# A three-stage kernel on one core: the low half of M taken by VectorE in block 0, and the conversion of the weights re-ordered

## The chip, the cores and the metric

One core of one Trainium2 chip runs the whole program. The time is in device microseconds of one execution, and lower is better. TensorE (PE) multiplies; ScalarE (ACT) and VectorE (DVE) work element by element; SyncE (SP) issues every transfer of this kernel. TensorE's clock is granted at one of two levels, 1.2 or 2.4 GHz; the profile gives it as 0.50 or 1.00.

## The reference

```python
scores  = scale * x @ state^T                 # B=8, H=8, S=512, Ns=32, D=64
xread   = softmax(scores) @ state             # tokens read the state
sread   = softmax(scores^T) @ x               # the state reads the tokens
x = concat([xread, sread]) as 4608 rows of 512
x = relu(x @ w_in)**2 @ w_out                 # first layer pair, 512 -> 2048 -> 512
y = elu(x @ w2_in) @ w2_out                   # second layer pair, 512 -> 2048 -> 512
```

The activations are 32-bit floats. The four weight matrices come as 64-bit floats, and the kernel makes 32-bit ones of them on the chip.

## The kernel before

**Precision.** TensorE multiplies numbers that are cut to fewer bits (fp32r). Each operand is therefore held as two such parts, a high one (`HI`) and a low one (`LO`, what the high one leaves over), and each product is made of three matmuls of 128x512: HI·LO, HI·HI, LO·HI (`mm3`, lines 168 to 172). `split` (line 174) makes the two parts: ScalarE copies the high part, VectorE subtracts it from the source.

**Blocks and steps.** The tokens are worked on in eight blocks of 512, one for each entry of the batch. Blocks 0 to 3 are the single stage. A block has 16 steps f, and each step (`s1_step`) makes a tile h of 128 hidden units by 512 tokens with six matmuls (`h<-at,m`), then relu and square on ScalarE (`relu2`: r, g and the high part of gs) and the low part of gs on VectorE. Two steps later (`LAG` is 2) `out_step` multiplies that gs with the output weights by twelve matmuls (`acc<-gs,v`). Blocks 4 to 7 are the pair stage: it begins with steps that make h for block 4 (`h_step`, line 737) and works in fewer products over pairs of blocks. The second layer pair comes last.

**M.** Instead of making x for a block and multiplying it with w1, the kernel multiplies state with w1 (M, in four groups g of four steps; `emit_m`, `m_heads`: 8 short matmuls `mp<-w,st`) and the attention weights with M. A group of M needs two units of w1, and steps 4g to 4g+3 need the group. In blocks 1 to 7 `split` makes M's two parts. In block 0 TensorE makes the low one: the high part is multiplied by minus one (tile `minus`) and added to the bank in which M stands, and ScalarE copies what is left (lines 374 to 376).

**Conversion of the weights.** Beside the blocks, `next_conv` advances a list of units (`converting`): w1 and v1 (8 units each, in block 0), then combinations of v1 (`sums_v1`), then w2 and v2 (`conv_pair`). A unit of `convert` (line 222) has two ScalarE instructions of 128x1024 (lines 232 and 234), three VectorE ones (236, 237, 240), and for v1 a high copy on ScalarE (256) and a subtraction on VectorE (258). Its transfers go through SyncE's queue. `wf` is the split result of a later unit (281, 282), written back to memory. What has not been converted when block 3 ends is done at once (`while busy or converting`, line 706).

**Order.** Each engine runs its instructions in a fixed order, which a scheduler writes down from the order of the code and from `issue_after` hints: inside such a context the instructions that go to the engine of the named instruction come behind it on that engine. `gate` and `pace` hold such instructions: `pace` is the last step's relu.

**The beginning.** `begin_block` does block 0's attention while the first weights arrive; `busy_pe(n)` puts n matmuls that compute nothing (`idle`) into TensorE's order. Two matmul records stand for one such matmul.

Of the kernel before, what the change touches and what calls it, by code (L numbers as in the profile page):

```python
# [8 lines left out]
F32 = mybir.dt.float32  # L9
F32R = mybir.dt.float32r  # L10
I32 = mybir.dt.int32
U32 = mybir.dt.uint32
AF = mybir.ActivationFunctionType
# [96 lines left out]
def attn_mlp_kernel(ctx: ExitStack, tc: tile.TileContext, xt, xn, st, w1, v1, w2, v2, outx, outs):  # L110
# [57 lines left out]
    def mm3(ps, w, x, first, last):  # L168
# [2 lines left out]
        mm(ps, w[HI], x[HI], start=False, stop=False)  # L171
        mm(ps, w[LO], x[HI], start=False, stop=last)  # L172

    def split(hi, lo, src):
        copy = nc.scalar.activation(out=hi, in_=src, func=AF.Copy)  # L175
        nc.vector.tensor_tensor(out=lo, in0=src, in1=hi.bitcast(F32), op=ALU.subtract)  # L176
        return copy

    x2d = [dram.tile([P, KC, S if b < B else NST], F32, name=f"x2d{b}", tag=f"x2d{b}") for b in range(B + 1)]
# [1 line left out]
    if True:  # L181
        ident = const.tile([P, P], F32, name="ident")
        make_identity(nc, ident)
        minus = const.tile([P, P], F32R, name="minus")
        nc.scalar.activation(out=minus, in_=ident, func=AF.Copy, scale=-1.0)
        stf = sf_p.tile([P, KC, NST], F32, name="stf", tag="stf")


# [33 lines left out]
        def convert(name, i, out):  # L222

            t = raw.pop((name, i))
            low, high = t[..., 0], t[..., 1]
            bits = out.bitcast(I32)
            after = pace if name in ("w2", "v2") else gate  # L230
            with tc.issue_after(after[0].ins) if after else nullcontext():
                nc.scalar.activation(out=out, in_=high.bitcast(F32), func=AF.Prelu, scale=2.0 ** -112, alpha=NEGATIVE)
            with tc.issue_after(gate[-1].ins) if gate else nullcontext():
                taken[:] = [nc.scalar.activation(out=low, in_=low.bitcast(U32), func=AF.Copy, scale=2.0 ** -29)]
            yield
            nc.vector.tensor_scalar(out=out, in0=out, scalar1=CLAMP, scalar2=-NEGATIVE * CLAMP, op0=ALU.min, op1=ALU.max)
            nc.vector.tensor_single_scalar(out=bits, in_=bits, scalar=3, op=ALU.logical_shift_left)
            yield
            for r in range(2) if (name, i) == ("w1", 1) else [slice(0, 2)]:
                added[name, i] = nc.vector.tensor_tensor(out=bits[:, r], in0=bits[:, r], in1=low[:, r], op=ALU.add)  # L240
# [8 lines left out]
        def conv_v1(i):  # L249
            v = conv_p["cv"].tile([P, 2, 512], F32, name="cv", tag="cv")  # L250
            yield from convert("v1", i, v)
            next_pair(reading)
            d = dram.tile([P, 2, 512], F32, name=f"d_v1{i}", tag=f"d_v1{i}")
            nc.sync.dma_start(out=d, in_=v)
            t = wo_p.tile([P, 2, 2, DM], F32R, name=f"v1_{i}", tag="wo")
            nc.scalar.activation(out=t[:, :, HI], in_=v, func=AF.Copy)
            yield
            nc.vector.tensor_tensor(out=t[:, :, LO], in0=v, in1=t[:, :, HI].bitcast(F32), op=ALU.subtract)
            for r in range(2):
                wd["v1", 2 * i + r], wo_t["v1", 2 * i + r] = d[:, r], t[:, r]  # L260
# [54 lines left out]

        v1d = {}
        wo_t = {}
        pieces = [("w1", 0), ("w1", 1), ("v1", 0), ("v1", 1)]
        for i in range(2, 8):
            pieces += [("w1", i), ("v1", i)]  # L320
        pairs2 = [(name, j) for name in ("w2", "v2") for j in range(HF)]
        converting = pieces + [("f1", j) for j in range(HF)] + pairs2[:IN_SINGLE]
        of_units = lambda units: [(name, i, r) for name, i in units for r in range(2)]
# [23 lines left out]
        def next_piece():  # L347
            next_conv(converting[0][0] in ("w1", "v1"))

        m_t, minus_copy = {}, []  # L350

        def heads(ps, b, x, ks=range(KC)):

# [5 lines left out]
        def m_heads(ps, b, g, ks):  # L359
            heads(ps, b, lambda k, r: half[g, k // 2][r, k % 2, :], ks)  # L360

        def emit_m(b, g):

            ps = [ps_aux.tile([P, 512], F32, name=f"mp{b}_{g}_{e}", tag="aux") for e in range(2)]
            m_heads(ps, b, g, range(KC))
            split_m(b, g, ps)

        def split_m(b, g, ps):
            for e in range(2):
                t = m_p.tile([P, 2, 512], F32R, name=f"m{b}_{g}{e}", tag="m")  # L370
                if b:
                    split(t[:, HI], t[:, LO], ps[e])
                else:
                    nc.scalar.activation(out=t[:, HI], in_=ps[e], func=AF.Copy)
                    mm(ps[e], minus, t[:, HI], start=False, stop=True, skip_group_check=True)
                    minus_copy[:] = [nc.scalar.activation(out=t[:, LO], in_=ps[e], func=AF.Copy)]
                m_t[b, g, e] = t

        A = {}
# [19 lines left out]
        def begin_block():  # L399

            act, tt, after = nc.scalar.activation, nc.vector.tensor_tensor, lambda i: tc.issue_after(i.ins)
            pss = [ps_aux.tile([P, 512], F32, name=f"sc0_{e}", tag="aux") for e in range(2)]
            with busy_pe(14):
                heads(pss, 0, lambda k, r: xt_t[0][r, k, :])
            load_xn(0)
            for queue in (reading, loading, reading):
# [15 lines left out]
            neg = nc.vector.tensor_scalar_mul(mx, mx, -SCALE)  # L422
            busy_pe(4)
            units = [conv_w1(i) for i in range(2)]
            del converting[:2]
            gate[:] = [last]
            next(units[0])
            gate.clear()
# [9 lines left out]
            next(units[1])  # L438
            gate[:] = taken
            unit = conv_v1(0)  # L440
            del converting[0]
            next(unit)
            gate.clear()
            A[0] = dict(t=t, e2=e2, z2=z2)
# [4 lines left out]
            next(units[0], None)  # L449
            last = added["w1", 0]  # L450
            m_heads(mps, 0, 0, (0, 1))
            busy_pe(6)
            a2t = A[0]["a2t"] = at_p.tile([P, ST, 2, P], F32, name="a2t0", tag="a2t")
            tp = ps_t.tile([P, ST, 2, P], F32, name="tp0", tag="pt")
            for s in range(ST):
# [11 lines left out]
            for c in range(2):  # L467
                for s in range(ST):
                    nc.tensor.transpose(atf[:, c, s * P:(s + 1) * P], back[:, c, s], ident)
            with after(last):  # L470
                next(units[1])
            next(units[1], None)
            m_heads(mps, 0, 0, (2, 3))
            operand(0)
            with after(copies[0]):
                split_m(0, 0, mps)
            next(unit)
            gate[:] = [copies[0], minus_copy[-1]]
            second = conv_v1(1)
            del converting[0]  # L480
            next(second)
            busy.append((second, "v1"))
            gate[:] = gate[1:]
            next(unit)
            next(unit, None)

        def at_soft1(b):

# [141 lines left out]
        def busy_pe(n):  # L630

            t = ps_s1.tile([P, 512], F32, name="idle", tag="s1")
            for i in range(n):
                last = mm(t[:, i % 4 * P:(i % 4 + 1) * P], ident, ident, start=True, stop=True, skip_group_check=True)
            return tc.issue_after(last.ins)
# [10 lines left out]
        for b in range(SINGLE):  # L646
            bg = {i: later.pop(i, []) for i in range(FC + LAG)}

            def at(i, fn, *a):
                bg[i].append(lambda: fn(*a))  # L650

            nb = b + 1
            if b == 0:
                for i in range(FC - 1):
                    at(i, next_piece)
                    at(i, next_conv, False)
                at(0, gate.clear)
                at(3, emit_m, 0, 1)
                at(7, emit_m, 0, 2)
                at(11, emit_m, 0, 3)  # L660
                at(1, at_sread, 0)
                at(2, at_srt, 0)
                at(2, load_x, 1)
            else:
                at(1, emit_m, b, 1)
                at(5, emit_m, b, 2)
                at(9, emit_m, b, 3)
                for i in range(18):
                    for _ in range(int(('111111211211111100', '111111212211211100')[b == 1][i])):
                        at(i, next_conv)  # L670
            at(13, emit_m, nb, 0)
            if nb < SINGLE:
# [501 lines left out]
```

## Time and profile before

| | |
|---|---|
| median of three runs | 1321.7 us (1320.56 to 1325.08) |
| the profiled execution, its time | 1325.68 us |
| its span, from the first to the last instruction | 1323.9 us |
| mean granted clock | 0.996 |
| PE, DVE, ACT busy in the span | 98%, 71%, 63% |

A row of a timeline gives the start in us from the span's start, the duration, the engine, the line, the operation, the tiles (out<-in), the shape and the count. In brackets stands how long the engine had been idle before, and what ended the wait. Successive starts are closer together than durations, since the next instruction begins before the last one has drained.

### The profile page before, as it was taken

The numbers are of one execution on the slowest core, as the hardware profiler recorded it, in microseconds if no ns is written. First come the engines' busy times: TensorE is split into PE (matmuls) and PEld (weight loads), VectorE is DVE, ScalarE is ACT, GpSimd is POOL, SyncE is SP. The second block draws the span as 40 slices with busy tenths as digits, with TensorE's granted clock in tenths as the row PEclk, the third lists the DMA queues.
The fourth block names the chain that finished last, engine by engine and source line by source line (L and its number), as shares of the span: only waits on it lengthen the run. The fifth ranks groups of instructions, "written<-read, shape, count | busy, mean of one in ns | idle before, by whom it ended". The sixth has DMA issues, their size and how long they took to land.

```text
span 1323.9 us, 19412 instructions
## 1 busy us (share of the span) xinstructions
PE 1302.3 (98%) x6972; PEld 1039.9 (79%) x6972; DVE 942.0 (71%) x1324; ACT 840.3 (63%) x1358; POOL 0.7 (0%) x6
## 2 busy tenths in 40 slices
PE   7999999999899999999999999999999999999999
PEld 5677777777577777778988888788888888888888
DVE  5984768787968965895856963689546984568645
ACT  6995677777776566654657743675446843666444
POOL 0000000000000000000000000000000000000000
PEclk8999999999999999999999999999999999999999
DMA  9788767778843663589676677777786677778733
GB/s 376 276 309 308 265 238 253 293 269 304 317 139 106 226 196 120 151 273 334 260 248 196 191 209 240 247 190 213 207 288 195 207 209 222 211 201 283 229 118 112
DMA packets 135408, 305.39 MB, mean 231 GB/s; under 512 B 14352, under 2 KB 28688, under 8 KB 132240
## 3 DMA queue, kind: packets, MB, share of 16 engines
q1 hardware_dynamic: 135312, 304.14, 70.6%
q8 instruction: 56, 0.92, 0.3%
q14 instruction: 40, 0.33, 0.1%
HBM read 227.54 MB, written 76.55 MB: 230 GB/s over the span
## 4 chain that ended last, share of the span: by engine, by line
PE 78%; DVE 9%; DMA 6%; ACT 2%; issue 2%; SPq 0%; ACTq 0%; DVEq 0%
PE x L43 19%; PE X L43 13%; PE z L43 9%; PE Z L43 6%; PE y L43 3%; PE acc L170 3%; PE h L170 3%; PE Y L43 3%; PE h L172 3%; PE h L171 3%; PE acc L172 3%; PE acc L171 3%; PE mp L357 2%; PE as L43 2%; PE hs L43 1%
## 5 line engine op out<-in xcount | busy, mean ns | idle before, releaser
L176 DVE TENSOR_TENSOR gp<-g,gp 128x512 fp32r<-128x512 f32 (+1 forms) x224 | 212.0, 955 | 106.4 <-ACT gp L175 105.4
L175 ACT ACTIVATE gp<-g 128x512 fp32r<-128x512 f32 (+1 forms) x224 | 187.2, 843 | 154.8 <-PE x L43 74.9
L43 PE MATMUL x<-gp,wr 128*128 128x512 f32 x1152 | 273.5, 391 | 1.4 <-DVE gp L176 1.4
L43 PEld LDWEIGHTS x<-gp,wr 128*128 128x128 f32 x1152 | 214.8, 188 | 53.0 <-DVE gp L176 4.1
L43 PE MATMUL X<-xf,wr 128*128 128x512 f32 x768 | 186.9, 390 | 1.0 <-ACT u L960 1.0
L43 PEld LDWEIGHTS X<-xf,wr 128*128 128x128 f32 x768 | 143.4, 188 | 32.9 <-ACT u L960 2.5
L43 PE MATMUL z<-gp,wr 128*128 128x512 f32 x576 | 133.5, 390 | 0.0
L43 PEld LDWEIGHTS z<-gp,wr 128*128 128x128 f32 x576 | 107.9, 188 | 23.5 <-issue 0.8
L956 DVE SCALAR_TENSOR_TENSOR g<-r,g 128x512 f32<-128x512 f32 x96 | 64.0, 689 | 62.8 <-ACT r L955 62.8
L170 PE MATMUL acc<-gs,v 128*128 128x512 f32 x256 | 103.7, 405 | 2.3 <-DVE gs L592 1.6
L170 PE MATMUL h<-at,m 128*128 128x512 f32 x256 | 102.5, 400 | 0.5 <-ACT g L746 0.5
L172 PE MATMUL h<-at,m 128*128 128x512 f32 x256 | 100.5, 394 | 0.0
L171 PE MATMUL h<-at,m 128*128 128x512 f32 x256 | 100.4, 393 | 0.0
L172 PE MATMUL acc<-gs,v 128*128 128x512 f32 x256 | 100.1, 391 | 0.0
L171 PE MATMUL acc<-gs,v 128*128 128x512 f32 x256 | 99.7, 389 | 0.0
L43 PE MATMUL Z<-xf,wr 128*128 128x512 f32 x384 | 97.6, 389 | 0.0
L954 ACT ACTIVATE r<-g 128x512 f32<-128x512 f32 x96 | 57.6, 625 | 60.3 <-DVE g L1004 43.6
L81 DVE TENSOR_TENSOR g<-g,g 128x1024 f32<-128x1024 f32 x72 | 87.5, 1220 | 0.8
L43 PEld LDWEIGHTS Z<-xf,wr 128*128 128x128 f32 x384 | 72.0, 188 | 15.2 <-DVE g L1010 0.3
L955 ACT ACTIVATE r<-r 128x512 f32<-128x512 f32 x136 | 81.5, 621 | 0.7
L170 PEld LDWEIGHTS acc<-gs,v 128*128 128x128 f32 x256 | 48.0, 188 | 29.8 <-issue 11.7
L43 PE MATMUL y<-gp,wr 128*128 128x512 f32 x288 | 68.6, 389 | 0.0
(169 smaller groups left out, 2002.1 us busy)
## 6 DMA issues: line engine op xcount, KB each, us to landing
wr<-f_v SPq DMA_DIRECT2D x288, 256.0 KB, 3.1
wr<-f_w SPq DMA_DIRECT2D x224, 256.0 KB, 3.0
f_v<-wf SPq DMA_DIRECT2D x40, 512.0 KB, 3.4
raw_w<-in_w_dram SPq DMA_DIRECT2D x32, 512.0 KB, 5.7
raw_v<-in_v_dram SPq DMA_DIRECT2D x32, 512.0 KB, 6.6
f_w<-wf SPq DMA_DIRECT2D x24, 512.0 KB, 3.3
wr<-p_v SPq DMA_DIRECT2D x48, 256.0 KB, 3.5
xt<-in_xt_dram SPq DMA_DIRECT2D x8, 1024.0 KB, 6.8
```

Source lines behind the costliest of these rows:

```text
L43: nc.tensor.matmul(ps, wk[a], xk[b], start=start and k == 0 and i == 0, stop=last and k == len(w) - 1 and i == 2, skip_group_check=True)
L81: return lambda jj: tt(out=out[jj], in0=a[jj], in1=b[jj], op=ALU.subtract)
L170: mm(ps, w[HI], x[LO], start=first, stop=False)
L171: mm(ps, w[HI], x[HI], start=False, stop=False)
L172: mm(ps, w[LO], x[HI], start=False, stop=last)
L175: copy = nc.scalar.activation(out=hi, in_=src, func=AF.Copy)
L176: nc.vector.tensor_tensor(out=lo, in0=src, in1=hi.bitcast(F32), op=ALU.subtract)
L357: mm(ps[e][32 * k:32 * k + 32, :], st_t[b][r, k, :], x(k, r), start=True, stop=True)
L954: act(out=r, in_=h, func=AF.Relu, scale=-1.0)
L955: act(out=r, in_=r, func=AF.Exp, scale=-1.0)
L956: nc.vector.scalar_tensor_tensor(out=out, in0=r, scalar=-1.0, in1=h, op0=ALU.add, op1=ALU.max)
```

## The change

Five things change. In block 0, as in the others, `split` makes both parts of M: the eight matmuls with `minus`, the tile itself and ScalarE's eight copies of a low part are gone, and VectorE gets eight subtractions. The unit that was converted ahead of step 0 as a second one of v1 now comes in its turn. All conversion copies of ScalarE, not those of w2 and v2 alone, stand behind the last step's relu. The high copies of v1's units 3 and 7 go to VectorE. The idle matmuls are dealt out otherwise (12, 4, 4, 4 for 14, 4, 6), M's heads take k in the order 2, 3, 0, 1, and block 1 advances the conversion 24 times instead of 20.

```diff
     def split(hi, lo, src):
         copy = nc.scalar.activation(out=hi, in_=src, func=AF.Copy)
-        nc.vector.tensor_tensor(out=lo, in0=src, in1=hi.bitcast(F32), op=ALU.subtract)
+        lows[:] = [nc.vector.tensor_tensor(out=lo, in0=src, in1=hi.bitcast(F32), op=ALU.subtract)]
...
-        minus = const.tile([P, P], F32R, name="minus")
-        nc.scalar.activation(out=minus, in_=ident, func=AF.Copy, scale=-1.0)
...
-            after = pace if name in ("w2", "v2") else gate
+            after = gate or pace
...
-            with tc.issue_after(gate[-1].ins) if gate else nullcontext():
+            with tc.issue_after(after[-1].ins) if after else nullcontext():
...
-            nc.scalar.activation(out=t[:, :, HI], in_=v, func=AF.Copy)
+            if i % 4 == 3:
+                nc.vector.tensor_copy(out=t[:, :, HI], in_=v)
+            else:
+                nc.scalar.activation(out=t[:, :, HI], in_=v, func=AF.Copy)
...
-        pieces = [("w1", 0), ("w1", 1), ("v1", 0), ("v1", 1)]
+        pieces = [("w1", 0), ("w1", 1), ("v1", 0)]
         for i in range(2, 8):
-            pieces += [("w1", i), ("v1", i)]
+            pieces += [("w1", i), ("v1", i - 1)]
+        pieces += [("v1", 7)]
...
-            m_heads(ps, b, g, range(KC))
+            m_heads(ps, b, g, (2, 3, 0, 1))
...
-                if b:
-                    split(t[:, HI], t[:, LO], ps[e])
-                else:
-                    nc.scalar.activation(out=t[:, HI], in_=ps[e], func=AF.Copy)
-                    mm(ps[e], minus, t[:, HI], start=False, stop=True, skip_group_check=True)
-                    minus_copy[:] = [nc.scalar.activation(out=t[:, LO], in_=ps[e], func=AF.Copy)]
+                split(t[:, HI], t[:, LO], ps[e])
...
-            with busy_pe(14):
+            with busy_pe(12):
...
-            busy_pe(6)
+            with after(last):
+                busy_pe(4)
...
             with after(last):
+                busy_pe(4)
                 next(units[1])
...
-            next(unit)
-            gate[:] = [copies[0], minus_copy[-1]]
-            second = conv_v1(1)
-            del converting[0]
-            next(second)
-            busy.append((second, "v1"))
-            gate[:] = gate[1:]
+            with after(lows[0]):
+                next(unit)
+            gate[:] = lows
             next(unit)
             next(unit, None)
+            gate.clear()
...
-                    for _ in range(int(('111111211211111100', '111111212211211100')[b == 1][i])):
+                    for _ in range(int(('111111211211111100', '222222111211211100')[b == 1][i])):
```

The scheduler moves more than the diff shows. Line numbers of the changed kernel are a few lower or higher for the same statement. Here is TensorE's order in the beginning, before the change, from the last matmul of block 0's scores (`sc`) to the first of its M (`mp`):

```order
L357 MATMUL sc_1_176<-xt_165,st_163 32x512
L634 MATMUL idle<-ident 128x128 x3
L420 MATMUL pt<-ident,sc_210 128x128 x8
L634 MATMUL idle<-ident 128x128 x7
L457 MATMUL tp_271<-ident,e_212 128x128 x3
L357 MATMUL mp_0_0_251<-w_0_235,st_163 32x512
```

And with the change:

```order
L361 MATMUL sc_1_174<-xt_163,st_161 32x512
L631 MATMUL idle<-ident 128x128 x10
L419 MATMUL pt<-ident,sc_206 128x128 x8
L631 MATMUL idle<-ident 128x128 x2
L456 MATMUL tp_265<-ident,e_208 128x128 x2
L361 MATMUL mp_0_0_247<-w_0_231,st_161 32x512
```

Seven of the idle matmuls (the new calls hint at a VectorE instruction, which orders nothing on TensorE) have moved ahead of the transposes `pt`, on which the softmax of block 0 waits.

VectorE's order in the changed kernel shortly before M's third group (`m_20`, `m_21`), where `cv` and `v_3` belong to units of v1, `w_5` to one of w1, `t` and `z` to the softmax of block 1:

```order
L257 CAST v_3_626<-cv 128x2x512
L237 TENSOR_SCALAR w_5_628<-w_5_628 128x1024
L261 TENSOR_TENSOR v_3_626<-cv,v_3_626 128x2x512
L489 TENSOR_REDUCE m_634<-t_573 128x32
L589 TENSOR_TENSOR gs<-g,gs 128x512
L490 TENSOR_TENSOR t_573<-t_573,m_634 128x1024
L240 ISA w_5_628<-raw_w_363,w_5_628 128x2048
L236 TENSOR_SCALAR cv<-cv 128x1024
L497 TENSOR_REDUCE z_691<-t_573 128x32
L237 TENSOR_SCALAR cv<-cv 128x1024
L240 ISA cv<-raw_v_157,cv 128x2048
L178 TENSOR_TENSOR m_20_685<-mp_2_0_675,m_20_685 128x512
```

Before, VectorE had no part in M in block 0; its order from the same unit of w1 on was:

```order
L237 TENSOR_SCALAR w_5_646<-w_5_646 128x1024
L396 STREAM_TRANSPOSE t_591<-sc_0_595 128x512
L396 STREAM_TRANSPOSE t_591<-sc_1_596 128x512
L240 ISA w_5_646<-raw_w_379,w_5_646 128x2048
L592 TENSOR_TENSOR gs<-g,gs 128x512
L258 TENSOR_TENSOR v_4_644<-cv,v_4_644 128x2x512
```

The low part of M now stands behind the whole of a v1 unit's three instructions, and the unit of w1 that M needs behind more of the softmax.

ScalarE's order where block 3 ends, before the change (`oo`, `o`: the block's result; `wf`: units of the conversion that are left; L746: the first relu of the pair stage, tile h_3575):

```order
L622 ACTIVATE oo<-acc 128x512
L622 ACTIVATE o<-acc 128x512
L281 ACTIVATE wf<-tf 128x2x256
L175 ACTIVATE m_10_3608<-mp_1_0_3598 128x512
L175 ACTIVATE m_11_3611<-mp_1_1_3599 128x512
...
L175 ACTIVATE m_20_3680<-mp_2_0_3670 128x512
L175 ACTIVATE m_21_3683<-mp_2_1_3671 128x512
L281 ACTIVATE wf<-cv 128x2x256
L281 ACTIVATE wf<-tf 128x2x256
L746 ACTIVATE g_3582<-h_3575 128x512
```

And with the change, where that relu is line 742:

```order
L619 ACTIVATE oo<-acc 128x512
L619 ACTIVATE o<-acc 128x512
L742 ACTIVATE g_3573<-h_3566 128x512
L746 ACTIVATE g_3573<-g_3573 128x512
L177 ACTIVATE gp<-g_3573 128x512
L742 ACTIVATE g_3573<-h_3580 128x512
L491 ACTIVATE t_3418<-t_3418 128x1024
L177 ACTIVATE m_10_3599<-mp_1_0_3589 128x512
```

The first relu of the pair stage has moved from behind thirteen other instructions to right behind the block's result.

## Rows read from the trace of the kernel before

**Rows 1.** The page: busy us (share of the span) xinstructions.
```profile
PE 1302.3 (98%) x6972; PEld 1039.9 (79%) x6972; DVE 942.0 (71%) x1324; ACT 840.3 (63%) x1358; POOL 0.7 (0%) x6
```

**Rows 2.** Windows: us, busy PE, PEld, DVE, ACT, POOL (xcount), clock, DMA share, GB/s.
```profile
20.00:30.00 10.00, 7.38 (x20) 4.17 (x21) 6.89 (x10) 7.65 (x11) 0.00 (x0) 0.53 1.02 409
...
70.00:80.00 10.00, 10.00 (x50) 8.38 (x49) 9.92 (x14) 10.00 (x16) 0.00 (x0) 1.00 0.85 302
```

**Rows 3.** TensorE's timeline, the beginning up to the first output product.
```profile
1.35 6.02 PE L634 MATMUL idle<-ident 128*128 128x128 f32 x28 [1.35 <-POOL ident masks.py:199]
...
10.12 1.73 PE L634 MATMUL idle<-ident 128*128 128x128 f32 x14
...
21.73 2.52 PE L357 MATMUL mp<-w,st 64*32 64x512 f32 x8 [1.92 <-DVE w L240]
25.14 0.79 PE L375 MATMUL mp<-m,minus 128*128 128x512 f32 x1 [0.89 <-ACT m L374]
25.73 0.63 PE L170 MATMUL h<-at,m 128*128 128x512 f32 x1
...
35.63 0.50 PE L170 MATMUL acc<-gs,v 128*128 128x512 f32 x1 [1.58 <-DVE gs L592]
```

**Rows 4.** TensorE's timeline: first products with M's groups 1, 2 and 3.
```profile
48.67 0.39 PE L170 MATMUL h<-at,m 128*128 128x512 f32 x1
...
68.10 0.39 PE L375 MATMUL mp<-m,minus 128*128 128x512 f32 x1
68.33 0.39 PE L170 MATMUL h<-at,m 128*128 128x512 f32 x1
68.55 0.39 PE L375 MATMUL mp<-m,minus 128*128 128x512 f32 x1
...
88.59 0.39 PE L170 MATMUL h<-at,m 128*128 128x512 f32 x1
```

**Rows 5.** ScalarE's timeline, one step with a unit of w1.
```profile
30.66 0.60 ACT L587 ACTIVATE r<-h 128x512 f32<-128x512 f32 x1 [0.56 <-PE h L172]
31.16 1.20 ACT L232 ACTIVATE w<-raw_w 128x1024 f32<-128x1024 f32 x1
32.23 0.64 ACT L589 ACTIVATE g<-r 128x512 f32<-128x512 f32 x1
...
33.27 1.13 ACT L234 ACTIVATE raw_w<-raw_w 128x1024 int32<-128x1024 uint32 x1
34.29 1.05 ACT L256 ACTIVATE v<-cv 128x1024 fp32r<-128x1024 f32 x1
```

**Rows 6.** VectorE's timeline, a unit of v1 and the low part of a gs.
```profile
27.64 0.69 DVE L236 TENSOR_SCALAR cv<-cv 128x1024 f32<-128x1024 f32 x1 [2.32 <-ACT cv L232]
28.37 0.69 DVE L237 TENSOR_SCALAR cv<-cv 128x1024 int32<-128x1024 int32 x1
29.20 1.23 DVE L240 CUSTOM_DVE_ANT_0 cv<-raw_v,cv 128x2048 uint16<-128x2048 uint16 x1
30.34 1.22 DVE L258 TENSOR_TENSOR v<-cv,v 128x1024 fp32r<-128x1024 f32 x1
...
34.90 0.68 DVE L592 TENSOR_TENSOR gs<-g,gs 128x512 fp32r<-128x512 f32 x1
```

**Rows 7.** TensorE's timeline from block 3's end to the fifth step of block 4.
```profile
346.14 1.25 PE L519 MATMUL tp<-ident,e 128*128 128x128 f32 x8 [0.46 <-DVE m L176]
348.30 2.05 PE L357 MATMUL mp<-w,st 64*32 64x512 f32 x16 [0.91 <-ACT a2t L520]
351.81 1.06 PE L357 MATMUL mp<-w,st 64*32 64x512 f32 x8 [1.45 <-DVE m L176]
353.38 0.50 PE L170 MATMUL h<-at,m 128*128 128x512 f32 x1 [0.51 <-ACT g L746]
...
354.97 1.04 PE L357 MATMUL mp<-w,st 64*32 64x512 f32 x2
```

**Rows 8.** ScalarE's timeline, the first relu of the pair stage.
```profile
352.75 0.58 ACT L746 ACTIVATE g<-h 128x512 f32<-128x512 f32 x1
```

More of the change, by code (lines that the diff above doesn't have):

```diff
@@ L172, in mm3 @@
         mm(ps, w[LO], x[HI], start=False, stop=last)
+    lows = []
     def split(hi, lo, src):
         copy = nc.scalar.activation(out=hi, in_=src, func=AF.Copy)
-        nc.vector.tensor_tensor(out=lo, in0=src, in1=hi.bitcast(F32), op=ALU.subtract)
+        lows[:] = [nc.vector.tensor_tensor(out=lo, in0=src, in1=hi.bitcast(F32), op=ALU.subtract)]
         return copy
@@ L348, in next_piece @@
             next_conv(converting[0][0] in ("w1", "v1"))
-        m_t, minus_copy = {}, []
+        m_t = {}
         def heads(ps, b, x, ks=range(KC)):
@@ L424, in begin_block @@
             units = [conv_w1(i) for i in range(2)]
-            del converting[:2]
+            del converting[:3]
             gate[:] = [last]
@@ L476, in begin_block @@
                 split_m(0, 0, mps)
-            next(unit)
-            gate[:] = [copies[0], minus_copy[-1]]
-            second = conv_v1(1)
-            del converting[0]
-            next(second)
-            busy.append((second, "v1"))
-            gate[:] = gate[1:]
+            with after(lows[0]):
+                next(unit)
+            gate[:] = lows
             next(unit)
             next(unit, None)
+            gate.clear()
         def at_soft1(b):
@@ L656, in attn_mlp_kernel @@
                     at(i, next_conv, False)
-                at(0, gate.clear)
                 at(3, emit_m, 0, 1)
```

## The prediction

> **What bounds the kernel now.** The page comes first: TensorE (PE) is busy for 98% of the span [rows 1], so a change can gain only where TensorE waits, where its clock is low, or where it is spared work. The windows by stage and TensorE's timeline show three such places. The first is the beginning: between 20 and 30 us the granted clock is 0.53, that is mostly the 1.2 GHz level [rows 2], after a time in which TensorE had little to do; it waits 1.92 us for a unit of w1, 0.89 for M's high copy, and 1.58 before the first output product at 35.63 [rows 3]. The second is the rest of block 0, where from 70 to 80 us VectorE is busy for 9.92 and ScalarE for 10.0 of 10 us while TensorE has no gap [rows 2]: there neither of the two can take on work without TensorE soon waiting for it. The third is the end of block 3. From 345.7 to 353.4 TensorE waits four times, 3.33 us in all, and the two short groups of M between take longer than their work [rows 7].
>
> **The change, the beginning.** A step's ScalarE work comes from its successive starts: relu 0.50, first conversion copy 1.07, g and gs 1.04 together, second copy 1.02, and for v1 a high copy of 0.95 to 1.05 [rows 5]. On VectorE a unit takes 0.73, 0.83 and 1.14, v1's subtraction 1.13 to 1.22, a low part of 512 columns 0.68 or a little less [rows 6]. A TensorE product starts every 0.225 us at full clock [rows 4]; at the lower level I take 0.45.
>
> The idle matmuls ahead of the scores are four records fewer, at 0.215 each [rows 3]: 0.85 us earlier at the most. I take 0.4, since the transfer of x then decides. Against that, fourteen more records stand before the transposes `pt`, 0.124 each at the later rate [rows 3], 1.7 us, part of it a wait for the copy anyway: `pt` and the softmax come some 0.9 later than now. VectorE's two steps of the first v1 unit, about 1.2 us, which stood between the softmax and the second unit of w1, now stand behind M. These three cancel to within 0.3 us, so M's heads start near 21.7 as now, and the first product h stands where the matmul with `minus` stood, at 25.0 instead of 25.73 [rows 3].
>
> From there: twelve products of steps 0 and 1 at 0.45 end at 30.2, the read of the state takes 1.1, and the six of step 2, mostly at full clock, end at 32.8. The first output product needs gs of step 0: relu at 28.65 (eight products after 25.0), 2.6 of ScalarE, 0.6 of VectorE, 31.9; and v1's high copy, 32.2. So it starts at 32.8 instead of 35.63. ScalarE is now the slow one. From 28.65 it has four steps without a gap, 4 x 3.63 + 2 x 0.95 = 16.4, then M's copy, and the first product with M's group 1 comes at 45.6. Before, it is at 48.67 [rows 4]. By the orders of the two programs 37 output products stand ahead of it before and 39 with the change; at equal work that is 48.67 + 2 x 0.225 - 45.6 = **3.5 us gained**.
>
> **The rest of block 0.** ScalarE is spared six more low copies (0.5 each) and two high copies of v1; VectorE gets six low parts (0.6 to 0.68) and the two high copies. No row shows such a copy on VectorE: its nearest are L236, one source and the same 1024 columns in 0.69, and L258, two sources in 1.22 [rows 6]. I take 0.69, since the copy has one source. The Trainium skill (VectorE: DVE Perf Modes, the perf-mode tier table) says that in 32 bits one-source operations between SBUF tiles run at twice the rate of two-source ones; with 1.22 the third group of M would come 0.55 later.
>
> By its order VectorE has in steps 4 to 7 four gs (2.6), two units of w1 (5.4), two of v1 (7.7), a high copy (0.7), two low parts of M (1.3) and about 6.5 of block 1's softmax: some 24 us against 18.6 of TensorE (72 products and the short groups). TensorE has output products in reserve, but it works them off. Going down the orders row by row with the durations above: the high copy of v1's unit 3 is ready at 60.4, wanted at 60.0; gs of step 7 0.6 late; M's group 2 at 67.95, where 96 output products have been done, against 78 at 68.33 before [rows 4]: 68.33 + 18 x 0.225 - 67.95 = 4.4 gained. Then `m_20`'s low part, queued behind a v1 unit's addition, holds TensorE for 1.6 (70.45 instead of 68.85), and behind it stand all further products. ScalarE's next four steps, from 71.55, have no gap: 4 x 3.63, two copies of 0.5 for the transposed weights, one of 0.5 of the operand, v1's 0.95 and M's 0.5 make 17.5, and group 3 comes at 89.0, with 136 output products done instead of 125 at 88.59 [rows 4]: 88.59 + 11 x 0.225 - 89.0 = 2.1. Conversion ends around 95 in both, from where TensorE alone decides; one more low part behind the last v1 unit leaves **1.8 us gained** at the end of block 0. Bounds: -2, if the hand-overs add a few tenths at each of a dozen waits, and 4.4, if the lag at group 3 is made up.
>
> **The end of block 3.** Before, the first relu of the pair stage runs at 352.75 [rows 8], though its product was ready when block 3 ended; it stands behind thirteen instructions, the leftover conversion among them. All banks for h are then full, so TensorE stands from 345.7 to 353.4, with 7.7 us for eight transposes (about 0.8), one full group of M (1.1) and half of another (1.06 by its row): 4.75 lost. Two groups are also cut in two, as the row at 354.97 shows (1.04 for two records, where the whole group needs 1.1) [rows 7]; in the new order they stand whole, 2.0 more. With the change the relu runs right behind the block's result. What is late next is M's group 1, behind an exponential on ScalarE, and its low parts behind two sums and a leftover piece on VectorE: I find waits of 0.4 to 1.9, and take 1.9. **4.85 us gained**; bounds 2 (the leftover still delays the softmax of block 5) and 6.4.
>
> **At nothing.** The 24 idle matmuls in all are as many as before. Block 1's four further advances lie in a stretch where ScalarE and VectorE are idle for a third and a fifth of the time. The raw words of v1's first four units are loaded before step 0 in both, and each later one is requested at least one step, 4 us, ahead of its copy; if that cover were gone, a transfer costs ScalarE what it waits.
>
> **The sum.** 1.8 + 4.85 = 6.7 us from the profiled execution's 1325.7 (its span 1323.9 and 1.8 around it): 1319.0. That execution is 0.3% above the median of the three runs shown, so the same share of the median gives 1321.7 x 1319.0 / 1325.7 = **1315 us**. About 0.3%, 4 us, is what a measurement of this kernel can tell from no change.
>
> **The rivals.**
> - VectorE and ScalarE eat up the whole gain of block 0. For it speak the full windows [rows 2]; against it the six low copies less on ScalarE. At the bound of -2 the sum is 2.85 and the time 1319. 0.17.
> - The clock rises later. In the beginning TensorE now has a gap between the idle matmuls and the scores, and only four idle records between the transposes and M instead of fourteen. If the scores, the twenty records and `pt` run at 1.2 GHz, they take some 3.5 longer, and the softmax of block 0 comes that much later: 6.7 - 3.5 leaves 3.2, 1318.5. Rows 3 speak against it, as 24 records still run without a gap before the scores. The Trainium skill (TensorE: Matmul & The Clock Gate, Part 4: PE-mode transpose) says that transposes do not count as activity for the clock; by that rule it would fall earlier here. No row tells transposes from the rest, though the clock did fall after a stretch that had mostly those. 0.10.
> - The end of block 3 does not get shorter: the wait moves from the relu to a transfer of the last converted pieces, whose tiles the pair stage's tiles replace. Before, such a transfer was one of the things waited for. Then 1.8 are left, 1320. 0.13.
> - Slower: VectorE decides all of block 0. Its work from gs of step 0 to group 3 is about 59 us; from 31.9 without idling it ends at 91. To lose 0.3% it must eat 4.85 + 4 on top of the 2.1 counted there, which is when it idles for 16% of that time, waiting for ScalarE in turn: then about 1326. Before, in 70 to 80 us, it idled for under 1% [rows 2]. 0.08.
>
> **How the numbers follow.** The forecast has 0.52, with 1311 to 1318 as its own range, nearly all of it faster by over 0.3%. The first two rivals reach below 1317.7 in about a third of their cases, which adds 0.08. So faster 0.58, within 0.3% 0.33, slower 0.09. The range goes from 1310.5, where block 0 gains 4.4 and the end of block 3 6.4, to 1321.5, where block 0 loses 2 and the end of block 3 gives 2; that leaves about 0.2 out.
>
> **What would show it.** In the profile of the changed kernel: the first output product near 32.8 and the first with M's group 1 near 45.6; a wait of TensorE for VectorE's low part of M in block 0 of one to two us; VectorE over 95% busy from 45 to 88; no gap of several us at the start of the pair stage, and its first relu within 2 us of block 3's result. The prediction is wrong if the first output product comes after 35, if block 0's short groups of M wait more than 3 us each, or if TensorE's idle time near 340 to 350 stays over 3 us.

## The result, and the profile after

The changed kernel takes 1312.5 us (median of five executions, 1311.6 to 1313.3), the kernel before in the same rounds 1325.0 (1320.6 to 1327.1): a ratio of 0.991, 95% interval 0.989 to 0.9935. The time is inside the predicted range, 2.5 us under the predicted 1315; the gain is 12.5 us, where the sum had 6.7. In the profiled executions the span went from 1323.9 to 1309.8, 14.1 us.

The page's line on the engines, to be laid beside [rows 1]:

```profile
PE 1291.3 (99%) x6964; PEld 1034.6 (79%) x6964; DVE 948.5 (72%) x1334; ACT 835.0 (64%) x1347; POOL 0.7 (0%) x6
```

The windows after, with the columns of [rows 2]:

```profile
15.00:20.00 5.00, 4.34 (x20) 2.37 (x21) 4.93 (x9) 5.00 (x9) 0.00 (x0) 0.66 1.02 412
...
20.00:30.00 10.00, 8.29 (x98) 5.18 (x97) 8.80 (x14) 7.23 (x12) 0.00 (x0) 1.00 1.02 396
45.00:88.00 43.00, 39.09 (x199) 27.21 (x199) 40.48 (x56) 37.71 (x55) 0.00 (x0) 1.00 0.87 316
60.00:70.00 10.00, 8.62 (x45) 5.29 (x46) 10.00 (x15) 5.25 (x8) 0.00 (x0) 1.00 0.86 295
70.00:80.00 10.00, 9.55 (x45) 7.37 (x43) 9.29 (x13) 10.00 (x15) 0.00 (x0) 1.00 0.94 381
```

From 20 to 30 us the granted clock is 1.00, where it was 0.53; it was low for 3.4 us before that (0.66 over 5 us). In block 0 TensorE now has gaps: VectorE fills 60 to 70 us while ScalarE is half idle, and ScalarE fills the next ten. The window from 45 to 88 us in the kernel before, to be laid beside the third row, shows which engine was relieved:

```profile
45.00:88.00 43.00, 42.41 (x212) 30.03 (x209) 39.92 (x55) 41.79 (x63) 0.00 (x0) 1.00 0.88 309
```

ScalarE went from 41.79 to 37.71 of 43 us, VectorE only from 39.92 to 40.48.

TensorE's timeline after: the beginning, the first products with M's groups 1 and 2, then the scores of block 2:

```profile
7.61 2.50 PE L631 MATMUL idle<-ident 128*128 128x128 f32 x20
9.95 1.04 PE L419 MATMUL pt<-ident,sc 128*128 128x128 f32 x8
...
15.32 0.33 PE L456 MATMUL tp<-ident,e 128*128 128x128 f32 x1 [3.89 <-ACT e L435]
...
16.24 1.93 PE L361 MATMUL mp<-w,st 64*32 64x512 f32 x8
...
23.71 0.50 PE L170 MATMUL h<-at,m 128*128 128x512 f32 x1 [0.68 <-ACT m L177]
...
29.58 0.50 PE L170 MATMUL acc<-gs,v 128*128 128x512 f32 x1 [0.25 <-ACT v L259]
...
43.13 0.40 PE L170 MATMUL h<-at,m 128*128 128x512 f32 x1
...
66.11 0.51 PE L170 MATMUL h<-at,m 128*128 128x512 f32 x1 [0.31 <-ACT m L177]
...
68.06 0.50 PE L172 MATMUL h<-at,m 128*128 128x512 f32 x1 [0.77 <-DVE m L178]
...
81.34 0.47 PE L170 MATMUL acc<-gs,v 128*128 128x512 f32 x1 [1.46 <-DVE gs L589]
...
86.82 0.49 PE L170 MATMUL h<-at,m 128*128 128x512 f32 x1
...
118.41 1.09 PE L361 MATMUL sc<-xt,st 64*32 64x512 f32 x16
```

And the end of block 3, to be laid beside [rows 7], with the first product behind it that takes a group of x:

```profile
326.63 1.18 PE L361 MATMUL sc<-xt,st 64*32 64x512 f32 x16
...
341.76 0.50 PE L172 MATMUL h<-at,m 128*128 128x512 f32 x1 [0.22 <-DVE m L178]
342.10 1.03 PE L516 MATMUL tp<-ident,e 128*128 128x128 f32 x8
...
344.45 1.30 PE L361 MATMUL mp<-w,st 64*32 64x512 f32 x16
...
351.35 1.09 PE L361 MATMUL mp<-w,st 64*32 64x512 f32 x16
...
364.81 1.52 PE L43 MATMUL x<-gp,wr 128*128 128x512 f32 x6
```

Where [rows 7] has four waits and two groups of M in pieces, one wait of 0.22 is left, and the groups stand whole. For the account, the same marks in the timeline of before:

```profile
122.25 1.09 PE L357 MATMUL sc<-xt,st 64*32 64x512 f32 x16
...
330.87 1.27 PE L357 MATMUL sc<-xt,st 64*32 64x512 f32 x16
...
376.11 1.52 PE L43 MATMUL x<-gp,wr 128*128 128x512 f32 x6
```

So at the first product with M's group 1 the changed kernel is ahead by 6.0 us (48.67 [rows 4] less 43.13, and two output products more done), at the scores of block 2 by 3.8, at those of block 5 by 4.2, at the first x by 11.3, at the end by 14.1.

### The profile page after: what moved, and what is told of

It is laid out like the page before. It is cut to its first block, busy times and chain, and to the rows that moved or that the text cites. A ratio compares the mean times of both kernels' runs of the same rounds, so it can differ in the third digit from the quotient of the medians.

```text
span 1309.8 us, 19385 instructions
## 1 busy us (share of the span) xinstructions
PE 1291.3 (99%) x6964; PEld 1034.6 (79%) x6964; DVE 948.5 (72%) x1334; ACT 835.0 (64%) x1347; POOL 0.7 (0%) x6
## 4 chain that ended last, share of the span: by engine, by line
PE 83%; DVE 8%; DMA 4%; ACT 3%; issue 2%; SPq 0%; POOLq 0%; DVEq 0%; ACTq 0%; POOL 0%
PE x L43 18%; PE X L43 13%; PE z L43 9%; PE Z L43 7%; PE y L43 4%; PE h L170 4%; PE h L172 4%; PE h L171 4%; PE acc L170 4%; PE Y L43 3%; PE acc L172 3%; PE acc L171 3%; PE mp L361 2%; PE as L43 2%; PE hs L43 1%
```

## The experiments

All compute the whole reference. Given are medians of five to twelve executions, with the shortest and the longest; each ratio is to the kernel before on the same chip, whose median was 1324.4 to 1325.6 in these rounds (1325.0 in the round of the result). So times of different runs can be compared to about a microsecond at best. A mark in a profile is one execution's, and the account below shows that two executions of the same work can differ by two microseconds at the beginning.

**1. Which part ends the gap at the end of block 3.** Theory A: the new string for block 1 deals the conversions out earlier, so that fewer are left behind the last relu. Theory B: it is the place of the copies behind the step's relu.

The string alone, in the kernel before:

```diff
-for _ in range(int(('111111211211111100', '111111212211211100')[b == 1][i])):
+for _ in range(int(('111111211211111100', '222222111211211100')[b == 1][i])):
```

> The kernel before with one edit of the change alone: the string that deals out background work in block 1, now 2 turns in each of its first six steps. Theory A (the end of block 3 is lost to leftover conversion copies, and the string alone moves them forward: four high copies are left behind the last relu where eight and a conversion were): the products of the pair stage start without the gap of rows 7, the span falls by about 7 us (the trace of after is 4.2 us ahead of before at the last scores of block 3 and 11.3 us ahead behind it), 1325.0 to about 1318, and the beginning and block 0 stand as before. Theory B (the gap goes because the copies wait behind the step's relu, the string only deals the work otherwise): no change within 2 us, 1323 to 1327, and rows 7 and 8 come back within 1 us of their lengths.

1319.25 us (1318.4 to 1320.2), ratio 0.995 (0.993 to 0.997). From the scores of block 5 to the first x it takes 38.3 us, where the kernel before takes 45.2 and the changed kernel 38.2; one wait is left between:

```profile
331.68 1.24 PE L357 MATMUL sc<-xt,st 64*32 64x512 f32 x16
...
346.41 0.50 PE L172 MATMUL h<-at,m 128*128 128x512 f32 x1 [0.67 <-DVE m L176]
...
369.96 1.30 PE L43 MATMUL x<-gp,wr 128*128 128x512 f32 x5
```

The copies' place alone, in the kernel before:

```diff
-after = pace if name in ("w2", "v2") else gate
+after = gate or pace
...
-with tc.issue_after(gate[-1].ins) if gate else nullcontext():
+with tc.issue_after(after[-1].ins) if after else nullcontext():
     taken[:] = [nc.scalar.activation(out=low, ...)]
```

> The kernel before with one edit of the change alone: every conversion copy is issued behind the step's relu. The leftover at the end of block 3 stays as long as before (eight high copies, one conversion). Theory A (leftover sets the gap): the gap at the end of block 3 stays at 4 to 6 us and the time stays within 3 us of 1325. Theory B (the place of the copies sets the gap): the gap is gone, about 1318. Beside it, on block 0: if the copies ahead of the relu were what kept ScalarE from the relus there, the waits of the acc products on gs fall and block 0 ends up to 2 us earlier.

1324.4 (1319.6 to 1329.2), ratio 0.9997 (0.998 to 1.001): no difference. The gap stands as before, 44.9 us on that way, with four waits of 3.3 us in all. The changed kernel with the old string, the edit of the first experiment backwards:

> The changed kernel with the old string for block 1; all else as changed. Theory A: the gap at the end of block 3 comes back in part or whole, and the time is 1312.5 + 7 = 1319.5 (1317 to 1321). Theory B: the copies are behind the relu here, so there is no gap, 1312.5 within 2 us. Up to the last scores of block 3 both expect the trace of the changed kernel to within 1 us.

1321.4 (1318.1 to 1324.6), ratio 0.997 (0.995 to 0.998): 8.9 over the changed kernel, more than A said. A holds and B falls: the copies are behind the relu here, and the gap is back, with 50.0 us from the scores of block 5 to the first x. Why it is longer still than before shows in the windows of this run and in its timeline behind the gap:

```profile
340.00:345.00 5.00, 3.56 (x24) 1.58 (x27) 4.82 (x9) 3.37 (x6) 0.00 (x0) 0.95 0.53 211
345.00:350.00 5.00, 3.60 (x19) 0.62 (x10) 4.54 (x12) 3.66 (x8) 0.00 (x0) 0.50 0.75 262
350.00:355.00 5.00, 5.00 (x14) 2.20 (x14) 4.29 (x7) 3.59 (x7) 0.00 (x0) 0.50 0.97 336
355.00:360.00 5.00, 5.00 (x17) 3.97 (x16) 1.29 (x2) 1.88 (x4) 0.00 (x0) 0.68 0.99 339
```

```profile
347.71 1.93 PE L361 MATMUL mp<-w,st 64*32 64x512 f32 x8 [1.40 <-DVE m L178]
349.57 0.79 PE L170 MATMUL h<-at,m 128*128 128x512 f32 x1
350.17 0.63 PE L171 MATMUL h<-at,m 128*128 128x512 f32 x1
350.59 0.63 PE L172 MATMUL h<-at,m 128*128 128x512 f32 x1
```

The products behind the gap start every 0.43 us, not 0.23: the clock fell to its lower level in the gap and came back at about 358. In the profiled execution of before it did not fall there.

**2. The two parts together.** With the string alone, the way from block 3's scores to block 4's (scores are made a block ahead, so it runs from the middle of block 2 to that of block 3) took 77.2 us, against 74.0 before (271.26 less 197.28): TensorE waited 0.8 there for a relu and 0.9 for a copy of block 2's result, both on ScalarE, and 0.5 for VectorE, where before it had no wait. Both edits of part 1 in the kernel before:

> The kernel before with two parts of the change: the new string for block 1, and every conversion copy issued behind the step's relu. Nothing else of block 0 is changed. Theory A2 (the string removes the gap at the end of block 3; copies ahead of the relu cost the run with the string alone another 3.2 us between the last scores of block 2 and of block 3, 77.2 us there where the kernel before takes 74.0): the two together give 1319.25 - 3.2 = 1316.0 (1315 to 1317.5), with 74.0 us there and no gap at the end of block 3. What is left to the changed kernel, some 3.5 us, is then the beginning and block 0. Rival: the 3.2 us come from the new string's own dealing and stay; 1319 within 1 us.

1315.2 (1312.9 to 1318.0), ratio 0.992 (0.990 to 0.994), and 74.0 us on that way (194.23 to 268.21). So behind the relu the copies are worth 4 us, but only with the new string; the two make 10 of the 12.5 us. What is left, 2.7 between the medians, is the beginning and block 0: at the scores of block 2 this run stands at 120.23, the changed kernel at 118.41.

**3. The parts of block 0,** each undone in the changed kernel. The cast on VectorE:

```diff
-if i % 4 == 3:
-    nc.vector.tensor_copy(out=t[:, :, HI], in_=v)
-else:
-    nc.scalar.activation(out=t[:, :, HI], in_=v, func=AF.Copy)
+nc.scalar.activation(out=t[:, :, HI], in_=v, func=AF.Copy)
```

> The changed kernel with all eight high copies of v1 on ScalarE (no cast on VectorE). Theory F (VectorE is now what holds block 0: it is busy 10.0 of 10 us from 60 to 70 us, where ScalarE is busy 5.25): two casts of 0.69 us less on VectorE let the low parts of M and of gs come earlier, block 0 ends 0.5 to 1.4 us earlier, 1311.1 to 1312.0. Rival (ScalarE's chain of relu, squares and copies sets each step): two copies of 1.07 us more on ScalarE, block 0 ends 1 to 2 us later, 1313.5 to 1314.5.

1312.1 (1311.3 to 1313.8): 0.5 less, within what can be told. So the casts on VectorE earn nothing that these runs show: the rival's loss did not come, and F's gain is not told apart from none. One unit of v1 ahead, undone:

```diff
-pieces += [("w1", i), ("v1", i - 1)]
+pieces += [("w1", i), ("v1", i)]
...
 gate[:] = lows
+second = conv_v1(1)
+next(second)
+busy.append((second, "v1"))
 next(unit)
```

> The changed kernel with two units of v1 ahead instead of one, as in the kernel before. Theory G (the second unit's four steps stand between M group 0 and group 1 on VectorE and ScalarE): M group 1 comes 1 to 2.5 us later than 43.1, and what is taken early there is given back later in block 0, so the end of block 0 moves by 0 to 1.5 us; 1312.5 to 1314. Rival (units of v1 are what the acc products wait for later): block 0 ends up to 1 us earlier, 1311.5.

1316.15 (1314.7 to 1316.7), ratio 0.992 (0.991 to 0.994): 3.6 over the changed kernel, more than G said, and the two sets of executions do not overlap; the second unit is worth nothing here. (By the ratios alone, 0.992 and 0.991, the two would not be told apart.) The waits of TensorE in this run begin:

```profile
PE acc L170 <- DVE gs L591: 5.3, 8, 1.3
PE tp L455 <- ACT e L434: 4.1, 2, 3.9
PE h L170 <- ACT m L177: 1.8, 2, 1.5
PE h L172 <- DVE m L178: 1.7, 3, 0.8
```

The output products wait eight times for VectorE's gs, 5.3 us, where the changed kernel has five times and 2.8. The scores of block 2 come at 122.36. In the run of part 2, with two units ahead too but M's low half by TensorE and ScalarE, they come at 120.23. The two runs differ in M's low half above all (in the cast, the idle matmuls and the order of M's heads too), so these two profiles say that with two units ahead the rest of the change makes the way to the scores of block 2 some 2 us longer. That is no more than two executions of one program can differ by, but the long wait is for the engine that got the low halves. M's low half as before, with one unit ahead:

```diff
+minus = const.tile([P, P], F32R, name="minus")
+nc.scalar.activation(out=minus, in_=ident, func=AF.Copy, scale=-1.0)
...
-split(t[:, HI], t[:, LO], ps[e])
+if b:
+    split(t[:, HI], t[:, LO], ps[e])
+else:
+    nc.scalar.activation(out=t[:, HI], in_=ps[e], func=AF.Copy)
+    mm(ps[e], minus, t[:, HI], start=False, stop=True, skip_group_check=True)
+    lows[:] = [nc.scalar.activation(out=t[:, LO], in_=ps[e], func=AF.Copy)]
```

> The changed kernel with the low half of M in block 0 made as before: by a product of TensorE with the negated identity and a second copy on ScalarE. Theory H (this is what the gain of block 0 consists of): each of four groups gets 2 products of 0.23 us and 2 copies of about 0.6 us on ScalarE back; group 0 at the beginning comes 0.5 to 1 us later, block 0 ends 2 to 4 us later, 1314.5 to 1316.5. Rival F2 (VectorE holds block 0 in the changed kernel, and the work taken from it there pays for what ScalarE gets): the end of block 0 within 1 us of the changed kernel's, 1311.5 to 1313.5.

1314.1 (1312.3 to 1315.4), ratio 0.991 (0.989 to 0.9925): 1.6 over the changed kernel by the medians, between the two theories, with executions that overlap and the same ratio. Its scores of block 2 are at 119.23, 0.8 later, but it starts with an advantage that part 5 shows. So no run here settles how much the low half on VectorE earns. The order in which M's heads take k was not undone in any run.

**4. The idle matmuls at the beginning,** as before: 14, 4 and 6 in place of 12, 4, 4 and 4.

> The changed kernel with the idle matmuls of before: 14 ahead of the scores, 4 behind pt, 6 ahead of the transposes of e, none ahead of the second heads of M group 0. Theory C (where the idle matmuls stand decides when the granted clock comes back to its upper level): the lower level lasts from about 16 to 20 us until 30 us or so as in the kernel before, the 12 first h products and the first acc products run at 0.45 us each, M group 1's first product comes some 2 to 3 us later than 43.1, and the time is about 1315. Theory D (the transposes and heads alone, in their new places, bring the clock back): the clock stands at 1.0 from 20 us on, and the time stays within 1 us of 1312.5.

1313.2 (1312.6 to 1315.1): 0.7 over, within what can be told. Theory C falls. D had the time but not the clock: from 20 to 30 us it is 0.88, and back at 1.0 before the first h product, at 24.00.

**5. What else taking out `minus` did.** Without it the order of TensorE has ten idle matmuls (20 records) between the scores and `pt`; `pt` starts at 9.95. An unused copy of the identity in its place brings the three back:

```diff
+warm = const.tile([P, P], F32R, name="warm")
+nc.scalar.activation(out=warm, in_=ident, func=AF.Copy)
```

> The changed kernel with one copy of the identity on ScalarE at the program's start, its result unused, where the kernel before made the negated identity. With it the order on TensorE puts 3 idle matmuls and not 10 between the scores and pt. Theory J (taking the negated identity out had a side effect: seven more idle matmuls stand ahead of pt, which starts at 9.95 us though ScalarE's copies of the scores end at 8.85, and VectorE waits 1.14 us for it): pt starts at 8.8, the first transpose of e at 14.4 (15.3 in the changed kernel), the first h product up to 0.9 us earlier than 23.7, and the time is 1311.6 to 1312.2. Rival (the copies of w1 behind the DMA set the first h product): the transposes come earlier, the first h product stays at 23.5 to 24, the time within 0.5 us of 1312.5.

1311.7 (1310.0 to 1314.0): 0.8 under the changed kernel, with executions that overlap. Its profiled execution was its slowest:

```profile
8.62 1.15 PE L421 MATMUL pt<-ident,sc 128*128 128x128 f32 x8
...
14.29 0.33 PE L458 MATMUL tp<-ident,e 128*128 128x128 f32 x1 [2.51 <-ACT e L437]
...
20.35 2.52 PE L363 MATMUL mp<-w,st 64*32 64x512 f32 x8 [1.05 <-DVE w L242]
23.55 0.80 PE L170 MATMUL h<-at,m 128*128 128x512 f32 x1 [0.68 <-ACT m L177]
24.14 0.63 PE L171 MATMUL h<-at,m 128*128 128x512 f32 x1
```

The transposes and the second heads of M start 1.0 earlier, as J says; but the clock fell at that place in this execution, the heads took 2.52 instead of 1.65, and the first product gained 0.16, as the rival had it. So this run shows the moved idle matmuls, not what they cost. With the casts on ScalarE too:

> The changed kernel with that early copy on ScalarE and with all high copies of v1 on ScalarE. Theory: the gains of the two add, 0.5 us (without the casts the median was 1312.06) and up to 0.9 us: 1311 to 1311.7. Rival: neither is real beyond 0.5 us, 1312 to 1312.8.

1310.25 (1309.4 to 1314.3), ratio 0.990 (0.988 to 0.992), 2.3 under the changed kernel by the medians, though its longest execution is longer than any of that one. The clock fell earlier here, the first h product is at 22.26, the scores of block 2 at 116.08.

**6. The clock.** Idle matmuls in the gap of the run with the old string:

```diff
+def fill(n, after):
+    t = ps_x.tile([P, S], F32, name="idle", tag="x")
+    with tc.issue_after(after().ins):
+        for i in range(n):
+            mm(t[:, i % 4 * P:(i % 4 + 1) * P], ident, ident, start=True, stop=True, skip_group_check=True)
...
 at(4 * q - 3, emit_m, b, q)
+if b == SINGLE and q == 2:
+    at(5, fill, 6, lambda: pe_last[-1])
...
 at(4, at_e2t, b + 1)
+at(4, fill, 5, lambda: pe_last[-1])
```

> The changed kernel with the old string for block 1 (as in the run with the old string) and eleven idle matmuls on TensorE in the gap at the end of block 3: five behind the transposes of e there, six behind the heads of M group 2. Nothing else is moved. Theory K (the gap costs twice: TensorE stands idle, and in some executions the granted clock falls to its lower level behind it, as from 344 to 358 us in the profile of the run with the old string; that makes the spread from 1318.1 to 1324.6): with TensorE kept busy the clock stands at 1.0 from 320 to 370 us, no execution has a mean clock under 0.996, and the time is 1318 to 1319.5 with a spread under 3 us. Rival (the spread and the time there come from the leftover copies or the DMA queues alone): the median stays at 1321 or above and the spread over 4 us.

1318.7 (1316.8 to 1323.4), 2.7 under the run with the old string, though the ratios of the two (0.996 and 0.997) have intervals that overlap. The windows there:

```profile
345.00:350.00 5.00, 3.67 (x38) 2.02 (x23) 4.99 (x13) 3.78 (x8) 0.00 (x0) 1.00 0.94 315
350.00:355.00 5.00, 5.00 (x25) 3.16 (x24) 4.38 (x7) 4.71 (x10) 0.00 (x0) 1.00 1.03 362
```

The clock stays up, and in all twelve executions its mean over the span is 0.996 to 0.999, against 0.992 to 0.997 without the idle matmuls. That part of K holds, and so does the time. The spread did not shrink as K said, 6.6 us: something besides the clock differs between executions with this gap, and stays open.

Eight more idle matmuls at the beginning, where TensorE waited 2.51 for the exponentials, on top of the kernel of part 5:

```diff
-            busy_pe(4)
+            busy_pe(12)
             units = [conv_w1(i) for i in range(2)]
```

> The kernel of the run without casts and with the early copy, and eight more idle matmuls between pt and the transposes of e, where TensorE waited 2.5 us for the exponentials on ScalarE; 17 of them take some 4.1 us and end at 13.3 us, ahead of the first transpose at 13.9. Theory K at the beginning (the clock falls after TensorE stood idle ahead of the transposes; one dip follows, of 3 to 10 us, at a place that differs between executions): with 0.5 us of idle in place of 2.5 the clock stands at 1.0 from 6 to 30 us, every execution has a mean clock of 0.999, the time is 1309.4 to 1310.3 and the spread falls from 4.9 us to under 2. Rival (the later idle stretches, ahead of pb and of the second heads of M group 0, or nothing on TensorE, decide it): a dip between 16 and 27 us remains, the mean clocks lie at 0.996 to 0.999 as before, and the median is 1310.2 to 1312.

1310.2 (1308.7 to 1311.3), ratio 0.9885 (0.987 to 0.990); none of its six executions is as long as the shortest of the changed kernel. But the median is that of the run it was built on (1310.25), so these idle matmuls show in the clock and in the spread, 2.7 us for 4.9, and not in the median. Four executions have a mean clock of 1.000, which no other kernel showed, and two 0.997. The profile is of one of these two:

```profile
15.00:20.00 5.00, 3.22 (x23) 1.74 (x23) 4.81 (x10) 5.00 (x7) 0.00 (x0) 1.00 1.01 410
20.00:25.00 5.00, 3.72 (x11) 1.34 (x12) 3.66 (x7) 2.43 (x5) 0.00 (x0) 0.60 1.03 409
```

So with the idle matmuls the fall seems rarer, and it still comes now and then, here behind two later waits (1.12 ahead of `pb`, 1.06 ahead of M's second heads): K has the fewer falls, the rival the dip that remains.

## Why the prediction was right, and where it was off

The three places and what happens at them were seen rightly; the sum was too small. It forecast a gain of 6.7 us, and 12.5 were measured. That the time is off by 2.5 us only is in part luck: it was counted down from 1321.7, the median of three executions, and the kernel before has a median of 1325.0 beside the changed kernel and 1324.4 to 1325.6 in the later rounds.

- **The beginning, 3.5 us: the mechanism held, the clock did not, and the size is not settled.** The first h product came at 23.71 (forecast 25.0), the first output product at 29.58 (32.8), M's group 1 at 43.13 (45.6), 6.0 us ahead. The step that failed is the lower clock until 30.2: the clock was back before 20. That is no merit of the change alone. The run with the string alone has the beginning of before, instruction for instruction, and its first product with M's group 1 at 46.63, not 48.67: 2.0 us that two executions of the same work differ by. Beside that run the gain is 46.63 - 43.13 + 2 x 0.225 = 3.95, near the 3.5, but there the scores start at 7.62 and in the changed kernel at 6.59. In the run of part 2, whose beginning is that of before but for the place of the conversion copies, the scores start at 6.62 and the mark is at 45.47 with 39 output products done: 2.3. So the gain here lies between 2.3 and the 6.0 of the two profiles, by what it is laid beside.
- **Block 0, 1.7 given back between group 1 and its end: held.** 6.0 fell to 3.8, so 2.2. At the scores of block 2 the changed kernel is ahead of the run with the string alone by 1.9 (120.27 less 118.41) and of the run of part 2 by 1.8, the 1.8 of the sum; the other two of the 3.8 are that difference between executions. M's group 2 came at 66.11 with 96 output products done, group 3 at 86.82 with 136: ahead by 6.3 and 4.2, where 4.4 and 2.1 were forecast, two us more, as at the beginning. Its low part held TensorE for 0.77 (forecast one to two), VectorE was busy for 94% from 45 to 88 us (over 95%). The cast took 0.69 (twice, 685 and 687 ns), as the row of one source and 1024 columns had it, and the subtraction of two sources over the same columns 1.2. By that the rule of the Trainium skill (VectorE: DVE Perf Modes, the perf-mode tier table), that one source goes at twice the rate of two, holds here as well.
- **Which edit earns it was seen wrongly.** The steps of v1 that now stand behind M went into the sum as 1.2 us that cancel. The term had the right size (with two units ahead the first h product comes at 24.94, 1.2 later), but what follows from it was missed: at the scores of block 2 that run is 3.95 behind, and 3.6 by the medians. The low halves on VectorE, credited with sparing ScalarE, seem to lose up to 2.1 us with two units ahead and to earn 0.8 to 1.6 with one; both figures are within what executions differ by. The two casts earned nothing that shows.
- **The end of block 3, 4.85: right in kind, too small.** The profile gives 7.1 (4.2 ahead at the scores of block 5, 11.3 at the first x). The mis-sized term is the 1.9 for new waits: 0.22 was measured, and 4.75 + 2.0 - 0.2 = 6.55 is what the other terms give; the last 0.5 was not located. The first relu of the pair stage runs at 334.88, 1.8 behind the start of block 3's last output product at 333.10. By the medians the gap is worth more still, 8.9 when it is put back, and 6.2 (1318.7 less 1312.5) when it is put back with idle matmuls that keep the clock up; so the clock, for which the sum had no term, may make some 2.7 of it.
- **Copies behind the relu: no term of their own.** Alone they change nothing, but without them the new string loses 3.2 us around the end of block 2. The forecast took them for granted.
- **Behind the first x** another 2.8 us were not forecast. Two waits of before, 1.4 for gp and 1.0 for u, are gone and one of 1.1 for eu is new; that makes 1.3. The rest was not located.
- **The rivals.** VectorE and ScalarE did not eat up block 0, the end of block 3 did get shorter, and the clock came back earlier, not later. What the Trainium skill says of transposes (TensorE: Matmul & The Clock Gate, Part 4), that they do not count as activity, was not told apart by any run: the clock did fall earlier than before (at about 16 in the profile of the changed kernel, at about 20.6 in that of before), but so it did with the old beginning, at about 14.4 in the run with the string alone; and the stretches with transposes after which it fell held waits as well.

## What to carry to other kernels

Work left over at a stage border is worth looking for ahead of the first wait that it causes, in a stretch where its engine is idle; and where it goes, it must stand behind what others wait for: here one edit alone gave 6 us, the other alone nothing, both 10. Between two full engines it paid little here to hand work over (the casts nothing, M's low halves 1.6 us at the most), and more to do less ahead of need (3.6). When an instruction goes, look at what the order of the others does: without `minus` seven more idle matmuls stood in front of the first softmax. And lay a profile beside a second one of the same program before a difference of a few microseconds is explained.

## What the runs showed of the hardware

TensorE's clock can fall after waits that are short each: in the run with the old string at about 344.5, after waits of 0.35 and 1.08 with TensorE busy for 3.56 of 5 us, and in the last run at about 21 after 0.73, 0.34, 1.12 and 1.06. It need not: in the profile of the kernel before, the waits of [rows 7] (0.46, 0.91, 1.45 and 0.51) brought no fall. Whether and where it falls differs between executions of one program, and each fall lasts 3 to 14 us here, at half speed. The Trainium skill (TensorE: Matmul & The Clock Gate, Part 1) says that the chip's look at TensorE's activity runs freely and does not start with the kernel, so that the moment of a change varies. That it varies agrees, with a fall at about 14.4 and one at about 20.6 us in two executions of the same beginning; the half microsecond that the section gives for a transition is far less than that. For the kernel before, the mean clock over the span lay between 0.991 and 0.997 in the 23 executions beside the first experiments and the time between 1321.6 and 1330.0; for the changed kernel 0.997 to 0.999 and 1311.6 to 1313.3. Where the clock fell in those executions no profile shows.
